# Batch 0's first loads on two queues: queries as fp32 by SP, keys as bf16 by POOL, and a new order of the first attention steps

## The chip, the cores and the metric

One Trainium2 chip, one core. The time is that of one execution on the device in microseconds; three runs are given by their median. Engines are called PE (TensorE), ACT (ScalarE), DVE (VectorE), POOL (GpSimd) and SP (SyncE); a load is issued by SP or by POOL and moved by the core's 16 DMA engines.

## The reference

Sliding-window attention over 8 batches of 8 heads, 576 positions of 64 elements, then two matrix products with a leaky ReLU between them:

```python
B, H, S, D = q.shape                      # 8, 8, 576, 64
scores = np.matmul(q, k.transpose(0, 1, 3, 2)) / np.sqrt(D)
mask = np.abs(pos[:, None] - pos[None, :]) <= 32
attn = softmax(np.where(mask, scores, -1e9))
x = np.matmul(attn, v).transpose(0, 2, 1, 3).reshape(B * S, H * D)   # 4608 x 512
h = x @ w_in                              # 512 x 2048
g = np.maximum(0.01 * h, h)
out = g @ w_out                           # 2048 x 512, float32
```

## The kernel before

Heads are worked in pairs, four pairs to a batch. For each pair, keys are laid out block-diagonally (`kbd`: head 0 in rows and columns 0 to 63, head 1 in 64 to 127, zeros elsewhere), so that one matmul serves both heads; values likewise in `vbd`. A step of attention is one pair and one half of the positions (288): five score matmuls into the PSUM tile `ps` (L296), an exponential on ACT (L301), the product with a 0/1 mask on POOL (L303, `prob`), row sums by a matmul with ones (L325, L328), their reciprocal on DVE (L333), five matmuls with the values (L347), and the scaling on DVE into `xT` (L361). Steps are numbered through: steps 0 to 3 are the four pairs of batch 0's first half, 4 to 7 its second half, and so on. After four steps 288 positions are ready for the first layer (`h_tile`, L375, and the activation at L382), and whole groups of 128 go through the second layer (`o_tile`, L417).

From batch 2 on, queries and keys are transposed by DMA, and a planner spreads the attention steps over the matmuls of the layers. Batches 0 and 1 are transposed on PE instead. The order of batch 0 is written out by hand (L481 to L532): each engine executes its instructions in the order of this text, so the place of a line decides what stands behind what in an engine's queue.

The queries and keys of batch 0 come by loads on POOL's queue that convert fp32 to bf16 on the way (`load_bf16`, L108): pairs 0 and 1 by themselves, pairs 2 and 3 in one load, queries and keys in turn. PE transposes them (L229), ACT evicts the queries into `qT` (L237). The keys of pairs 0 and 1 are evicted by ACT into `kT` (L250) and copied from there into `kbd` by DVE (`place_keys`, L279); those of pairs 2 and 3 go straight from PSUM into `kbd` by two ACT instructions (L245). The values come as fp32 by SP (L93, behind a small memset at L91) and are cast into `vbd` by POOL (L211) or ACT (L209). The parts of `kbd` and `vbd` that stay zero are cleared by DVE memsets (L143 to L147) and an ACT copy (L134).

`keep_busy` (L429) issues matmuls whose results nobody uses, so that PE doesn't stand still. The weights come by converting loads on POOL's queue (L475, L479). Batch 1's queries and keys are loaded by SP as fp32 (L79), behind a one-element memset on POOL (L75) that stands after the first two loads of w_out; they are cast to bf16 by DVE and POOL (L202) before PE transposes them (L232).

Of the kernel before, what the change touches and what calls it, by code (L numbers as in the profile page):

```python
# [9 lines left out]
FP32 = mybir.dt.float32  # L10
BF16 = mybir.dt.bfloat16
AF = mybir.ActivationFunctionType
# [4 lines left out]
def kernel(  # L17
# [14 lines left out]
    nc = tc.nc  # L32

    B, H, S, D = q.shape
# [52 lines left out]
    def load_v(b, p, behind=None):  # L87

        t = fload.tile([128, NB, D], FP32, name=f"vf{p}")
        if behind is not None:  # L90
            behind.memset(t[0:1, 0, 0:1], 0.0)  # L91
        for a in range(2):
            nc.sync.dma_start(  # L93
                out=t[64 * a:64 * a + 64],
                in_=v[b, 2 * p + a].rearrange("(c p) d -> p c d", p=64),
            )
        vf[b, p] = t
# [2 lines left out]
    kb = const.tile([96, NPAIR, RUN, 2, D], BF16)  # L100
    early = {}

    def load_bf16(p, n):

        for which, src in (("q", q), ("k", k)):
            t = (qb if which == "q" else kb)[:, p:p + n].rearrange("p n c a d -> p (n c a d)")
            t = t.rearrange("p (a c d) -> p a c d", c=RUN, d=D)
            nc.gpsimd.dma_start(  # L108
                out=t, in_=src[0, 2 * p:2 * (p + n)].rearrange("a (p c) d -> p a c d", c=RUN),
            )  # L110
            for i in range(n):
                early[which, p + i] = t[:, 2 * i:2 * i + 2]

    ident_f = const.tile([128, 128], FP32)
    make_identity(nc, ident_f)
    load_bf16(0, 1)
    load_bf16(1, 1)
    load_bf16(2, 2)
    ident = const.tile([128, 128], BF16)
    zero = const.tile([128, 1], BF16)  # L120
    nc.vector.memset(zero, 0.0)
# [10 lines left out]
    def clear(t, p):  # L132
        flat = t[:, p].rearrange("p n j -> p (n j)")
        nc.scalar.activation(  # L134
            out=flat, in_=zero.to_broadcast([128, NB * 128]), func=AF.Copy,
        )
# [5 lines left out]
    nc.vector.memset(win[0:64], 1.0)  # L142
    nc.vector.memset(kbd[0][:, 0:2], 0.0)  # L143
    nc.vector.tensor_copy(out=ident, in_=ident_f)
    nc.vector.memset(kbd[0][:, 2:4], 0.0)
    for p in range(1, NPAIR):
        nc.vector.memset(vbd[0][:, p], 0.0)  # L147

    WIN = [
        [((0, 0, 48), (2, 48, 64), (4, 112, 32)), ((1, 16, 64), (3, 80, 64))],  # L150
# [9 lines left out]
        out=w, in_=w, compare_op=ALU.is_ge, fill=0.0,  # L160
        base=2 * W, channel_multiplier=1, pattern=[[-1, 2], [0, 3], [-2, 64]],
    )
    win_f = win.rearrange("p c m i -> p c (m i)")

    def make_mask(hf):
# [12 lines left out]
        out=ps[:, 512:512 + HALF], in_=zero.to_broadcast([128, HALF]), func=AF.Copy,  # L178
    )
    clear(vbd[0], 0)  # L180


    RING = 4 * HALF
# [20 lines left out]
    def cast_v(b, p, eng=None, heads=range(2)):  # L204
        eng = eng or nc.gpsimd
        for a in heads:
            r = slice(64 * a, 64 * a + 64)
            if eng is nc.scalar:
                eng.activation(out=vbd[b % 2][r, p, :, r], in_=vf[b, p][r], func=AF.Copy)  # L209
            else:  # L210
                eng.tensor_copy(out=vbd[b % 2][r, p, :, r], in_=vf[b, p][r])  # L211
# [12 lines left out]
    def transpose(b, p, which):  # L224
        tp = mmps.tile([128, RUN, 96], BF16, name="tp", tag="mm")
        for c in range(RUN):
            if b == 0:
                for a in range(2):
                    nc.tensor.transpose(tp[64 * a:64 * a + 64, c], early[which, p][:, a, c], ident[0:96, 0:96])  # L229
            else:  # L230
                src = (qb if which == "q" else kb)[:, p, c].rearrange("p a d -> p (a d)")
                nc.tensor.transpose(tp[:, c], src, ident[0:96, 0:96])  # L232
        return tp

    def evict(b, p, which, tp, straight=False):
        if which == "q":
            nc.scalar.activation(  # L237
                out=qT[b][:, p].rearrange("p (c i e) -> p c i e", c=2, e=RUN // 2),
                in_=tp.rearrange("p (e c) i -> p c i e", c=2), func=AF.Copy,
            )  # L240
        elif straight:

            for a in range(2):
                r = slice(64 * a, 64 * a + 64)
                nc.scalar.activation(  # L245
                    out=kbd[b % 2][r, p, :, r], in_=tp[r].rearrange("p c i -> p i c"), func=AF.Copy,
                )
        else:
            kT = kt.tile([128, S], BF16, name="kT")
            nc.scalar.activation(  # L250
                out=kT.rearrange("p (i c) -> p i c", c=RUN),
                in_=tp.rearrange("p c i -> p i c"), func=AF.Copy,
            )
            unplaced.append((b, p, kT))

    def turn_over(b, p, which, straight=False):
        evict(b, p, which, transpose(b, p, which), straight)

    def transposes(b):

# [8 lines left out]
    def place_keys():  # L269

        while landing and landing[0][0] <= state["done"]:
            unplaced.append(landing.pop(0)[1:])
        while unplaced:
            b, p, kT = unplaced.pop(0)
            for a in range(2):
                r = slice(64 * a, 64 * a + 64)
                to = kbd[b % 2][r, p, :, r]
                if b < BY_DMA:
                    nc.vector.tensor_copy(out=to, in_=kT[r].rearrange("p (n j) -> p n j", j=64))  # L279
                else:  # L280
                    nc.vector.tensor_copy(  # L281
                        out=to.rearrange("p n (m c) -> p n c m", c=2),
                        in_=kT[r].rearrange("p (c n m) -> p n c m", c=2, n=NB),
                    )
# [6 lines left out]
    def score(i):  # L291
        b, hf, p = where(i)
        by_c = qT[b][:, p].rearrange("p (c i) -> p c i", c=2)
        for n_, blocks in enumerate(WIN[hf]):
            for blk, i0, n in blocks:
                nc.tensor.matmul(  # L296
                    ps_v[:, n_, :, i0:i0 + n], kbd[b % 2][:, p, blk],
                    by_c[:, :, hf * EVEN + i0:hf * EVEN + i0 + n], start=True, stop=True,
                )
        e = attn.tile([128, 2 * HALF], BF16, name="e")  # L300
        nc.scalar.activation(out=e, in_=ps[:, P0:P0 + 2 * HALF], func=AF.Exp, scale=scale)  # L301
        pr = prob[:, i % NPROB]
        nc.gpsimd.tensor_mul(  # L303
            pr.rearrange("p n c i -> p (n c i)"), e, mask[hf].rearrange("p n c i -> p (n c i)"),
        )
        probs[i] = [pr, None, None]
# [29 lines left out]
    def product(i, spare=False):  # L336

        b, hf, p = where(i)
        pr = probs[i][0]
        if spare:  # L340
            x = mmps.tile([128, 512], FP32, name="mm", tag="mm")[:, 0:HALF]
        else:
            x = xps.tile([128, HALF], FP32, name="x")
        x_v = x.rearrange("p (c i) -> p c i", c=2)
        parts = [(n_, *block) for n_ in range(2) for block in WIN[hf][n_]]
        for n_, blk, i0, n in parts:
            nc.tensor.matmul(  # L347
                x_v[:, :, i0:i0 + n], vbd[b % 2][:, p, blk, :], pr[:, n_, :, i0:i0 + n],
                start=(blk == parts[0][1]), stop=(blk == parts[-1][1]), skip_group_check=True,
            )  # L350
        probs[i][1] = x
# [7 lines left out]
    def scaled(i):  # L359
        _, x, r = probs.pop(i)  # L360
        nc.vector.tensor_mul(place(i), x, r)  # L361
# [63 lines left out]
    def keep_busy(t, lo, n):  # L425


        for _ in range(n):
            nc.tensor.matmul(  # L429
                t[:, lo:lo + 224], ones_bd, mask[0].rearrange("p n c i -> p (n c i)")[:, 0:224], start=False, stop=False,  # L430
                skip_group_check=True,
            )
# [41 lines left out]
    def load_w_in(f0, f1):  # L474
        nc.gpsimd.dma_start(out=w_in_bf[:, :, f0:f1], in_=w_in_r[:, :, f0:f1])  # L475
# [3 lines left out]
        nc.gpsimd.dma_start(out=w_out_bf[:, c, :], in_=w_out_r[:, c, :])  # L479

    qT[0] = attn.tile([128, NPAIR, S], BF16, name="qT")  # L481
    turn_over(0, 0, "q")
    turn_over(0, 0, "k")
    place_keys()
    for p in range(NPAIR):
        load_v(0, p, nc.vector if p == 0 else None)
    nc.vector.tensor_copy(out=win[64:128], in_=win[0:64])
    make_mask(0)
    turn_over(0, 1, "q")
    turn_over(0, 1, "k")  # L490
    score(0)
    place_keys()
    make_mask(1)
    turn_over(0, 2, "q")
    score(1)
    tq3 = transpose(0, 3, "q")
    turn_over(0, 2, "k", True)
    sums(0)
    evict(0, 3, "q", tq3)
    tk3 = transpose(0, 3, "k")  # L500
    keep_busy(ps, 0, 6)
    sums(1, True)
    load_w_in(0, 512)
    load_w_in(512, 1024)
    score(2)
    evict(0, 3, "k", tk3, True)
    keep_busy(ps, 0, 6)
    cast_v(0, 0, None, (0,))
    cast_v(0, 0, nc.scalar, (1,))
    cast_v(0, 1, None, (0,))  # L510
    cast_v(0, 1, nc.scalar, (1,))
    cast_v(0, 2, None, (0,))
    sums(2)
    score(3)
    product(0)
    product(1, True)
    scaled(0)
    scaled(1)
    cast_v(0, 2, nc.scalar, (1,))
    load_w_in(1024, 1536)  # L520
    keep_busy(ps, 0, 6)
    score(4)
    product(2)
    scaled(2)
# [149 lines left out]
```

## Time and profile before

| | |
|---|---|
| median of 3 runs | 321.42 us (321.33 to 322.27) |
| the profiled execution | 321.34 us, span of the instructions 319.6 us |
| batch 0's first query pair landed | 4.93 us |
| first score matmul | 9.46 us |
| first matmul of the first layer | 22.83 us |
| first issue of batch 1's loads | 26.51 us |

Times inside the run are microseconds from the start of the span. In a timeline a row is: start, duration, engine, line, operation, output <- input, and the number of instructions merged into it; in brackets the idle time of the engine ahead of it and what ended that. In a list of waits the three numbers are the total, how often, and the longest. PEld is PE's loading of weights, which runs beside its matmuls.

### The profile page before, as it was taken

Reading aid. Unit: us, or ns where it says so; the run is one execution under the profiler, and the core shown is the slowest. Engines: PE = TensorE matmul, PEld = TensorE weight load, DVE = VectorE, ACT = ScalarE, POOL = GpSimd, SP = SyncE. Lnnn points to the kernel's source line nnn. Section 1 sums busy time; section 2 is a strip of 40 time slices with the busy share of each in tenths; the row PEclk is TensorE's granted clock in tenths of the full one; section 3 lists DMA queues with packets and bytes.
Section 4 is the critical chain, followed back from the end, with each engine's and each line's share of the span. In section 5 each row is a group of like instructions: output and inputs, shape, how many; then the busy total and the mean of one; then the engine's idle time right before and its main releaser. Section 6 shows DMA issues by size and latency. Waiting matters only on the chain.

```text
span 319.6 us, 6565 instructions
## 1 busy us (share of the span) xinstructions
PE 305.3 (96%) x2498; PEld 205.7 (64%) x2498; DVE 216.2 (68%) x263; ACT 180.6 (56%) x391; POOL 187.5 (59%) x246
## 2 busy tenths in 40 slices
PE   1889988999999999999999999999999999999995
PEld 1677764576765858576765858576765858576753
DVE  6678645869755997688755997688755987565100
ACT  5677688574652828374552828365552828463631
POOL 7579845974646866586646866586646866330000
PEclk9999999999999999999999999999999999999999
DMA  6999999996999999399834998399733520000101
GB/s 86 191 154 175 267 254 210 242 218 144 214 246 182 226 245 180 77 206 231 177 74 95 262 191 177 77 243 207 162 76 106 113 63 35 35 35 7 61 33 67
DMA packets 108368, 48.28 MB, mean 151 GB/s; under 512 B 68784, under 2 KB 103856, under 8 KB 108336
## 3 DMA queue, kind: packets, MB, share of 16 engines
q1 hardware_dynamic: 102480, 42.48, 64.3%
q0 software_dynamic: 5856, 5.37, 11.1%
q8 instruction: 19, 0.31, 0.4%
q14 instruction: 13, 0.11, 0.1%
HBM read 36.70 MB, written 9.44 MB: 144 GB/s over the span
## 4 chain that ended last, share of the span: by engine, by line
PE 84%; DMA 8%; POOL 3%; SPq 1%; ACT 1%; issue 1%; DVE 1%; POOLq 0%; ACTq 0%; DVEq 0%
PE mm L417 37%; PE mm L375 34%; DMA kf<-in_k_dram 6%; PE x L347 4%; PE ps L296 4%; DMA qb<-in_q_dram 2%; PE s L325 2%; SPq L79 1%; POOL prob L303 1%; PE tp L229 1%; DVE r L333 1%; POOL w_in_bf L475 0%; POOL w_out_bf L479 0%; POOL qb L108 0%; ACT vbd L209 0%
## 5 line engine op out<-in xcount | busy, mean ns | idle before, releaser
L333 DVE RECIPROCAL r<-s 128x288 f32<-128x288 f32 x63 | 123.3, 1956 | 58.8 <-PE s L325 53.4
L303 POOL TENSOR_TENSOR prob<-e,mask 128x576 bf16<-128x576 bf16 x64 | 81.5, 1273 | 92.0 <-ACT e L301 45.4
L375 PE MATMUL mm<-xT,w_in_bf 128*128 128x288 bf16 x1024 | 134.0, 286 | 0.3
L417 PE MATMUL mm<-w_out_bf,gT 128*128 128x512 bf16 (+2 forms) x592 | 130.4, 373 | 0.2 <-DMA w_out_bf<-in_moe_w_out_dram 0.2
L382 ACT ACTIVATE gT<-mm 128x288 bf16<-128x288 f32 x256 | 101.2, 411 | 24.9 <-PE mm L375 8.4
L375 PEld LDWEIGHTS <-w_in_bf 128*128 128x128 bf16 x1024 | 98.4, 98 | 24.8 <-issue 0.6
L417 PEld LDWEIGHTS <-gT 128*128 128x128 bf16 x592 | 56.4, 98 | 59.6 <-issue 0.3
L422 ACT ACTIVATE o_sb<-mm 128x512 f32<-128x512 f32 (+2 forms) x37 | 21.7, 585 | 92.0 <-PE mm L417 92.0
L301 ACT ACTIVATE e<-ps 128x576 bf16<-128x576 f32 x64 | 41.5, 648 | 10.5 <-PE ps L296 10.3
L211 POOL CAST vbd<-vf 64x576 bf16<-64x576 f32 x51 | 35.1, 689 | 1.4
L202 POOL CAST kb<-kf 96x384 bf16<-96x384 f32 (+1 forms) x52 | 30.5, 608 | 5.7 <-DMA kf<-in_k_dram 5.7
L361 DVE TENSOR_TENSOR xT<-x,r 128x288 bf16<-128x288 f32 x63 | 28.8, 457 | 7.1 <-PE x L347 0.8
L281 DVE COPY kbd<-kT 64x576 bf16<-64x576 bf16 x48 | 32.3, 673 | 0.7 <-DMA kT<-kb 0.3
L296 PEld LDWEIGHTS <-kbd 128*128 128x128 bf16 x320 | 21.2, 100 | 8.9
L296 PE MATMUL ps<-qT,kbd 128*128 128x128 bf16 (+2 forms) x320 | 26.7, 216 | 0.0
L347 PE MATMUL x<-prob,vbd 128*128 128x64 bf16 (+1 forms) x315 | 25.6, 213 | 0.6 <-ACT vbd L209 0.4
L202 POOL CAST qb<-qf 96x384 bf16<-96x384 f32 x48 | 24.4, 536 | 0.0
L347 PEld LDWEIGHTS <-vbd 128*128 128x128 bf16 x320 | 20.8, 99 | 3.1 <-ACT vbd L209 0.7
L313 DVE TENSOR_TENSOR both<-prob 128x288 bf16<-128x288 bf16 x52 | 19.8, 382 | 0.9
L325 PE MATMUL s<-both,ones_bd 128*128 128x288 bf16 x52 | 14.9, 286 | 0.0
L229 PE MATMUL tp<-ident,qb 96*64 96x96 bf16 x48 | 2.8, 282 | 7.5 <-DMA qb<-in_q_dram 7.5
L209 ACT ACTIVATE vbd<-vf 64x576 bf16<-64x576 f32 x13 | 8.8, 680 | 0.3
(56 smaller groups left out, 86.3 us busy)
## 6 DMA issues: line engine op xcount, KB each, us to landing
vf<-in_v_dram SPq DMA_DIRECT2D x64, 144.0 KB, 4.5
out_dram<-o_sb SPq DMA_DIRECT2D x35, 256.0 KB, 4.0
qf<-in_q_dram SPq DMA_DIRECT2D x28, 288.0 KB, 4.7
kf<-in_k_dram SPq DMA_DIRECT2D x28, 288.0 KB, 5.1
w_in_bf<-in_moe_w_in_dram POOLq DMA_DIRECT2D x4, 512.0 KB, 6.7
w_out_bf<-in_moe_w_out_dram POOLq DMA_DIRECT2D x4, 512.0 KB, 16.3
qT<-qb SPq DMA_TRANSPOSE x24, 4.1
kT<-kb SPq DMA_TRANSPOSE x24, 3.2
```

What stands on the lines that cost most here:

```text
L202: eng.tensor_copy(out=to, in_=tok)
L211: eng.tensor_copy(out=vbd[b % 2][r, p, :, r], in_=vf[b, p][r])
L281: nc.vector.tensor_copy(out=to.rearrange("p n (m c) -> p n c m", c=2), in_=kT[r].rearrange("p (c n m) -> p n c m", c=2, n=NB),)
L296: nc.tensor.matmul(ps_v[:, n_, :, i0:i0 + n], kbd[b % 2][:, p, blk], by_c[:, :, hf * EVEN + i0:hf * EVEN + i0 + n], start=True, stop=True,)
L301: nc.scalar.activation(out=e, in_=ps[:, P0:P0 + 2 * HALF], func=AF.Exp, scale=scale)
L303: nc.gpsimd.tensor_mul(pr.rearrange("p n c i -> p (n c i)"), e, mask[hf].rearrange("p n c i -> p (n c i)"),)
L333: nc.vector.reciprocal(r, s)
L347: nc.tensor.matmul(x_v[:, :, i0:i0 + n], vbd[b % 2][:, p, blk, :], pr[:, n_, :, i0:i0 + n], start=(blk == parts[0][1]), stop=(blk == parts ...
L361: nc.vector.tensor_mul(place(i), x, r)
L375: nc.tensor.matmul(h[:, 0:HALF], w_in_bf[:, c, ts(f, 128)], xT[:, c, ds(g * HALF % RING, HALF)], start=(c == 0), stop=(c == DMC - 1),)
L382: nc.scalar.activation(out=gT[:, f, ds(g * HALF % RING, HALF)].rearrange("p (i c) -> p i c", c=2), in_=h[:, 0:HALF].rearrange("p (c i) -> ...
L417: nc.tensor.matmul(o[:, lo:hi], gT[:, f, ds(128 * j % RING, 128)], w_out_bf[:, f, lo:hi], start=(f == 0), stop=(f == FFC - 1),)
```

## The change

Batch 0's queries are no longer converted by the load. Four loads on SP's queue, one for each pair, bring them as fp32 into `qf`, and a new function `cast_q` casts them into `qb`: pairs 0 to 2 on DVE, pair 3 on POOL. The keys stay converting loads on POOL's queue, now one for each pair. Queries are therefore transposed with both heads in one instruction, keys as before one head at a time.

All keys of batch 0 go straight from PSUM into `kbd` (`straight`), pairs 0 and 1 by ACT and DVE with one head each, pairs 2 and 3 by ACT alone. Clearing moves: DVE clears `kbd`'s pairs 2 and 3 after the first query cast; `vbd`'s pair 1 goes to ACT, its pairs 2 and 3 to POOL.

The order of the first steps changes: the sums of step 0 stand ahead of the last transposes, the casts of values move to other engines and places, w_in's first load is issued after step 0 and its second after step 2, and three of the calls of `keep_busy` issue four matmuls instead of six.

```diff
-    def load_bf16(p, n):
-        for which, src in (("q", q), ("k", k)):
-            t = (qb if which == "q" else kb)[:, p:p + n].rearrange("p n c a d -> p (n c a d)")
-            t = t.rearrange("p (a c d) -> p a c d", c=RUN, d=D)
-            nc.gpsimd.dma_start(
-                out=t, in_=src[0, 2 * p:2 * (p + n)].rearrange("a (p c) d -> p a c d", c=RUN),
-            )
-            for i in range(n):
-                early[which, p + i] = t[:, 2 * i:2 * i + 2]
+    def load_early(p):
+        t = fload.tile([96, 2, RUN * D], FP32, name=f"qf{p}")
+        nc.sync.dma_start(out=t, in_=q[0, 2 * p:2 * p + 2].rearrange("a (p c) d -> p a (c d)", c=RUN))
+        qf[0, p] = t
+        t = kb[:, p].rearrange("p c a d -> p (c a d)").rearrange("p (a c d) -> p a c d", c=RUN, d=D)
+        nc.gpsimd.dma_start(out=t, in_=k[0, 2 * p:2 * p + 2].rearrange("a (p c) d -> p a c d", c=RUN))
+        early[p] = t
...
-    load_bf16(0, 1)
-    load_bf16(1, 1)
-    load_bf16(2, 2)
+    for p in range(NPAIR):
+        load_early(p)
...
-    nc.vector.memset(kbd[0][:, 2:4], 0.0)
-    for p in range(1, NPAIR):
-        nc.vector.memset(vbd[0][:, p], 0.0)
...
+    nc.gpsimd.memset(vbd[0][:, 2], 0.0)
+    nc.gpsimd.memset(vbd[0][:, 3], 0.0)
...
     clear(vbd[0], 0)
+    clear(vbd[0], 1)
...
+    def copy(eng, out, in_):
+        if eng is nc.scalar:
+            eng.activation(out=out, in_=in_, func=AF.Copy)
+        else:
+            eng.tensor_copy(out=out, in_=in_)
+
+    def straight(p, tp, *engs):
+        for a, eng in enumerate(engs):
+            r = slice(64 * a, 64 * a + 64)
+            copy(eng, kbd[0][r, p, :, r], tp[r].rearrange("p c i -> p i c"))
+
+    def cast_q(p, eng):
+        copy(eng, qb[:, p], qf[0, p].rearrange("p a (c d) -> p c a d", d=D))
...
+    ACT, DVE, POOL = nc.scalar, nc.vector, nc.gpsimd
+    cast_q(0, DVE)
     turn_over(0, 0, "q")
-    turn_over(0, 0, "k")
-    place_keys()
+    tk0 = transpose(0, 0, "k")
+    DVE.memset(kbd[0][:, 2:4], 0.0)
+    cast_q(1, DVE)
+    straight(0, tk0, ACT, DVE)
+    turn_over(0, 1, "q")
     for p in range(NPAIR):
-        load_v(0, p, nc.vector if p == 0 else None)
-    nc.vector.tensor_copy(out=win[64:128], in_=win[0:64])
+        load_v(0, p, DVE if p == 0 else None)
+    cast_q(2, DVE)
+    cast_q(3, POOL)
+    DVE.tensor_copy(out=win[64:128], in_=win[0:64])
     make_mask(0)
-    turn_over(0, 1, "q")
-    turn_over(0, 1, "k")
     score(0)
-    place_keys()
+    straight(1, transpose(0, 1, "k"), ACT, DVE)
+    turn_over(0, 2, "q")
     make_mask(1)
-    turn_over(0, 2, "q")
+    load_w_in(0, 512)
     score(1)
-    tq3 = transpose(0, 3, "q")
-    turn_over(0, 2, "k", True)
     sums(0)
-    evict(0, 3, "q", tq3)
+    straight(2, transpose(0, 2, "k"), ACT, ACT)
+    turn_over(0, 3, "q")
     tk3 = transpose(0, 3, "k")
-    keep_busy(ps, 0, 6)
+    keep_busy(ps, 0, 4)
     sums(1, True)
-    load_w_in(0, 512)
+    cast_v(0, 0, POOL, (0,))
+    score(2)
+    keep_busy(ps, 0, 4)
+    straight(3, tk3, ACT, ACT)
+    cast_v(0, 0, POOL, (1,))
     load_w_in(512, 1024)
-    score(2)
-    evict(0, 3, "k", tk3, True)
-    keep_busy(ps, 0, 6)
-    cast_v(0, 0, None, (0,))
-    cast_v(0, 0, nc.scalar, (1,))
-    cast_v(0, 1, None, (0,))
-    cast_v(0, 1, nc.scalar, (1,))
-    cast_v(0, 2, None, (0,))
     sums(2)
     score(3)
     product(0)
+    scaled(0)
+    cast_v(0, 1, ACT)
+    cast_v(0, 2, ACT, (0,))
+    cast_v(0, 2, POOL, (1,))
     product(1, True)
-    scaled(0)
     scaled(1)
-    cast_v(0, 2, nc.scalar, (1,))
     load_w_in(1024, 1536)
-    keep_busy(ps, 0, 6)
+    keep_busy(ps, 0, 4)
     score(4)
     product(2)
     scaled(2)
```

More of the change, by code (lines that the diff above doesn't have):

```diff
@@ L226, in transpose @@
         for c in range(RUN):
-            if b == 0:
+            if b == 0 and which == "k":
                 for a in range(2):
-                    nc.tensor.transpose(tp[64 * a:64 * a + 64, c], early[which, p][:, a, c], ident[0:96, 0:96])
+                    nc.tensor.transpose(tp[64 * a:64 * a + 64, c], early[p][:, a, c], ident[0:96, 0:96])
             else:
@@ L233, in transpose, with evict @@
         return tp
-    def evict(b, p, which, tp, straight=False):
+    def copy(eng, out, in_):
[9 more added lines that the diff above has]
+        copy(eng, qb[:, p], qf[0, p].rearrange("p a (c d) -> p c a d", d=D))
+    def evict(b, p, which, tp):
         if which == "q":
@@ L240, in evict @@
             )
[L241 to L247, printed above, removed]
         else:
@@ L254, in evict, with turn_over @@
             unplaced.append((b, p, kT))
-    def turn_over(b, p, which, straight=False):
-        evict(b, p, which, transpose(b, p, which), straight)
+    def turn_over(b, p, which):
+        evict(b, p, which, transpose(b, p, which))
     def transposes(b):
```

## The prediction

> **What bounds the kernel now.** The page's first part says which engine carries the run: PE is busy for 305.3 of 319.6 us, so a gain or loss must be PE time that is empty or slow now.
>
> ```profile
> PE 305.3 (96%) x2498; PEld 205.7 (64%) x2498; DVE 216.2 (68%) x263; ACT 180.6 (56%) x391; POOL 187.5 (59%) x246
> ```
>
> The list of PE's waits says where it is empty:
>
> ```profile
> PE tp L229 <- DMA qb<-in_q_dram: 7.5, 3, 5.0
> PE tp L232 <- POOL kb L202: 1.1, 2, 0.9
> PE ps L429 <- ACT e L301: 0.8, 1, 0.8
> PE x L347 <- ACT vbd L209: 0.4, 1, 0.4
> PE mm L417 <- DMA w_out_bf<-in_moe_w_out_dram: 0.2, 1, 0.2
> ```
>
> The first row is the 7.5 us that the change is about: batch 0's transposes waiting for queries. The second, fourth and fifth rows lie between 44 and 52 us: 0.89 + 0.20 + 0.44 + 0.21 = 1.74 us in which PE waits for batch 1's keys and values and the last of w_out. After that it waits no more, and every microsecond of shift reaches the end. So the prologue's end counts only as far as those transfers come earlier too. The chain that ended last shows what releases them: POOL's weight loads, POOL's small memset at L75, SP's issues at L79, and the last key load.
>
> ```profile
> 24.93 1.49 POOL w_out_bf L479 x2
> 26.42 0.07 POOL qf L75
> ...
> 30.45 17.78 DMA kf<-in_k_dram
> ```
>
> The engines' timelines, 16 to 27 us, give the steps from the third score on:
>
> ```profile
> 16.16 0.66 PE L296 MATMUL ps<-qT,kbd 128*128 128x96 bf16 x5
> 17.62 1.28 PE L429 MATMUL ps<-mask,ones_bd 128*128 128x224 bf16 x6 [0.80 <-ACT e L301]
> 20.31 0.66 PE L347 MATMUL mm<-prob,vbd 128*128 128x96 bf16 x5
> 21.55 0.40 PE L296 MATMUL ps<-qT,kbd 128*128 128x64 bf16 x5
> ```
>
> ```profile
> 18.78 1.25 ACT L209 ACTIVATE vbd<-vf 64x576 bf16<-64x576 f32 x2
> 20.16 0.65 ACT L301 ACTIVATE e<-ps 128x576 bf16<-128x576 f32 x1
> ```
>
> ```profile
> 17.65 1.27 POOL L303 TENSOR_TENSOR prob<-e,mask 128x576 bf16<-128x576 bf16 x1 [1.83 <-ACT e L301]
> 18.87 1.87 POOL L211 CAST vbd<-vf 64x576 bf16<-64x576 f32 x3
> 20.89 1.27 POOL L303 TENSOR_TENSOR prob<-e,mask 128x576 bf16<-128x576 bf16 x1
> 22.11 0.80 POOL L475 DMA_DIRECT2D w_in_bf<-in_moe_w_in_dram  x1
> ```
>
> To be seen here: ACT's and POOL's casts of the values fill the hole between one exponential and the next; five score matmuls take 0.66 us at first and 0.40 from 21.55 on, so PE runs at about half speed until some 21.15; and from 20.89 to SP's first issue at 26.51 POOL hardly pauses.
>
> **Part by part: the loads.** Six issues on POOL (0.63 to 0.82 each) become four, ended by 4.3 instead of 5.6. SP issues four fp32 query loads, 0.4 to 0.5 each (as L79), from about 0.8, when the other engines start. The eight pair loads of before moved packets from 3.3 (POOL's first issue at 1.58 plus 1.7) to the landing at 12.70: 9.4 us. From SP the stream can start at about 2.4.
> Does a second queue add speed? The windows by time show the engines already full: DMA share 1.12 at 6 to 8 us with POOL's queue alone, 1.15 at 38 to 40 us with both. So 9.4 us of work from 2.4 ends at 11.8: 0.9 us won, not half the time.
> How the two queues share isn't shown for this pair. If SP's stream goes first, the last query lands at 2.4 + 9.4/2 = 7.1; if last, at 11.8. In the packet records of 34 to 44 us the two queues advance packet for packet (about 110 each per us). With 1.2 us alone at the start, that puts the last query at some 9.6, the first keys at 5.6 (5.73 now). I take this.
>
> **Casts, evictions, memsets.** New are four casts of queries: three on DVE (0.56 alone, 1.24 beside a POOL memset, by L202) and one on POOL (0.82). The first keys go from PSUM to kbd by ACT's half (0.65, as L245) beside DVE's half. No row has that DVE copy: 0.46 is half of L279's pair out of SBUF, 0.92 twice L361's 288 columns out of PSUM; PSUM being the source, I take 0.75. ACT's eviction and DVE's two copies go (0.65 + 0.91 and two handovers), so the first score moves from 9.46 to about 8.1. DVE's moved memsets lie in its waits for data; two vbd memsets of 1.0 to 1.2 each go to POOL, whose queue ends them at about 7.7, before the last query lands. Should that landing be 7.1, they cost up to 0.6.
>
> **The new wait.** cast_q(3) stands on POOL ahead of the first probability product, and everything queued behind that: w_in's first issue, the second product, the casts of values. The sum, with the last query at 9.6: cast to 10.45, first product to 11.72 (10.93 to 12.20 now). sums(0) now stands ahead of the last three groups of transposes, so PE waits for that product with all of them behind it: sums(0) at 11.8, 0.5; three groups at 0.6, to 14.1; four keep_busy at 0.18 (1.09 for six now), to 14.8; sums(1) 0.48; score(2) at **15.3** instead of 16.16, a gain of 0.9. With the last query at 7.1, masks and score(1) bound instead: 14.2 or a little less. With 11.8: 17.5.
>
> **What follows score(2).** It sets the exponential of score(3) to end 4.65 us later, as now (20.81 − 16.16). But the casts of pair 1's values, done by 20.1 now, stand behind that exponential on ACT: two at 0.68, so product(1) runs 6.05 after score(2), not 4.15. PE queues keep_busy, score(4), product(2) and the first h matmul behind it. On POOL, one more cast (0.66) stands behind the fourth product, and the fifth waits for score(4): product 1.27 from 4.73, cast to 6.64, w_in's issue to 7.44; score(4) at 7.23 with PE slow, its exponential to 8.63, product to 10.0, w_in to 10.8, two w_out issues to 12.3, memset, SP's issue at 12.4 (11.6 with PE fast), against 10.35 now. Batch 1's first load is thus issued at 15.3 + 12.4 = 27.7 instead of 26.51: **1.2 us late**; with PE fast, 0.4. The idle DMA engines of now (share 0.44 at 22 to 24 us) get a second hole, since w_in's last quarter is issued at 25.3, not 24.14.
>
> **PE's speed.** PE is unbroken from 17.62 and speeds up 3.5 us later. After the change it stops for 1.9 us ahead of product(1) (21.35), so I count those 3.5 us from there, to 24.85: 3.5 us at half speed instead of 0.84, a loss of 1.3 us. Bounds: 0 if the stop doesn't count, 3.0 if another such stretch is needed.
> The Trainium skill (TensorE: Matmul & The Clock Gate, section "Part 1: The HAM clock gate (the "warmup" mystery)") has full speed come after a sustained busy window of about 3.4 us. The trace's 17.62 to 21.15 agrees, but 11.04 to 16.83 was as unbroken and released nothing; by the rule alone the sums after 11.8 could release it before the stop, and PE's sum below would be 0.9 instead of 2.2; the forecast would stay, since the transfers are later than either.
>
> **The sum on PE:** product(1) later by 21.35 − 20.31 = 1.04, two keep_busy fewer −0.19, half speed +1.33: first layer 2.2 later. The waits of 1.74 absorb that down to 0.4, but only if the transfers are no later; they are late by up to 1.2, and the chain of waits has them last. I take 1.2. On the profiled execution's 321.34 (span 319.6 and 1.74 around it) this is 322.54; the median of the runs is 0.08 higher: **322.6**.
>
> **The rivals.**
> *Queries first, faster:* SP's stream is served ahead of the keys, so POOL's cast leaves early, and sums(0) ahead of the transposes starts the chain early. It decides from score(2) before 14.3 on with PE fast by product(2): at 13.5 the load issue is at 13.5 + 11.6 = 25.1, 1.4 early, and PE's own sum is under the waits: 320.0. For it: SP starts 0.8 us ahead of POOL. Against: the packet-for-packet sharing, and score(1) behind mask and cast on DVE.
> *Hidden both ways, no change:* batch 1's first packet comes 4.4 us after its issue now, behind w_in's last quarter; a later issue may just wait less, and PE's loss goes into the 1.74: 321.5.
> *Late queries:* the last query at 11.8, or a second slow stretch of PE (2.2 + 1.7 − 1.74): 323.4 to 324.8; say 324.
>
> **How the numbers follow.** My forecast 0.38, late queries 0.12, no change 0.27, queries first 0.23. A measurement of this kernel can tell about 0.3%, 1 us. The forecast lies near that edge, so 0.03 of it goes to "same": slower 0.47, same 0.30, faster 0.23. The range reaches from near the fast rival to near the late one: 320.1 to 324.0; the forecast's own is 322.0 to 323.4.
>
> **What would show it.** Right: cast_q(3) waiting on POOL for a load until 9 to 10.5; score(2) near 15.3; PE idle nearly 2 us ahead of product(1), ended by ACT's cast; five-matmul groups still at 0.66 there; SP's batch-1 issue after 27; waits between 44 and 52 us shrunk. Wrong: cast_q(3) before 8.5, score(2) before 14.3, or SP's issue before 26.5.

## The result, and the profile after

The changed kernel takes **324.51 us** (median of 5 executions, 323.54 to 325.16) against 321.53 for the kernel before beside it: ratio 1.0087, 95% interval 1.0062 to 1.0112. It is slower by 3 us. The profiled execution took 323.54 (span 321.8), the shortest of the five, so the trace explains 2.2 of the 3 us; the rest lies in executions without a trace.

PE is busy for about as long as before (304.6 us for 305.3), so the loss is again empty or slow PE time.

```profile
PE 304.6 (95%) x2448; PEld 206.2 (64%) x2468; DVE 218.2 (68%) x261; ACT 181.4 (56%) x392; POOL 190.7 (59%) x247
```

The list of PE's waits (in total, times, longest):

```profile
PE tp L229 <- DVE qb L236: 4.4, 1, 4.4
PE tp L226 <- DMA kb<-in_k_dram: 2.0, 1, 2.0
PE ps L301 <- DVE kbd L236: 1.9, 2, 0.9
PE mm L352 <- ACT vbd L206: 1.6, 1, 1.6
PE x L352 <- ACT vbd L206: 0.9, 1, 0.9
```

The wait for queries is shorter, but three new ones stand below it: for keys, for DVE's half of their copy into `kbd`, and for ACT's cast of the values. After 44 us PE waits once, 0.94 us (the last line), where it waited 1.74 before. PE's timeline (start, length, work, and in brackets the idle time ahead of it):

```profile
7.04 0.69 PE L226 MATMUL tp<-ident,kb 96*64 96x96 bf16 x12 [1.98 <-DMA kb<-in_k_dram]
...
9.27 0.64 PE L301 MATMUL ps<-qT,kbd 128*128 128x96 bf16 x5 [0.94 <-DVE kbd L236]
...
16.14 0.66 PE L301 MATMUL ps<-qT,kbd 128*128 128x96 bf16 x5
...
22.11 0.63 PE L352 MATMUL mm<-prob,vbd 128*128 128x96 bf16 x5 [1.62 <-ACT vbd L206]
...
27.34 0.66 PE L301 MATMUL ps<-qT,kbd 128*128 128x64 bf16 x5
...
29.35 0.40 PE L301 MATMUL ps<-qT,kbd 128*128 128x64 bf16 x5
```

The first keys are turned at 7.04, not 5.78; the third score is where it was (16.16); product(1) comes 1.8 us later than before, behind a stop of 1.62; five score matmuls still take 0.66 us at 27.34, so PE is slow some 7 us longer. The other engines:

```profile
7.77 0.64 ACT L234 ACTIVATE kbd<-tp 64x576 bf16<-64x576 bf16 x1 [2.02 <-PE tp L226]
...
20.14 0.65 ACT L306 ACTIVATE e<-ps 128x576 bf16<-128x576 f32 x1 [1.41 <-PE ps L301]
20.69 2.08 ACT L206 ACTIVATE vbd<-vf 64x576 bf16<-64x576 f32 x3
```

```profile
8.45 0.76 DVE L236 COPY kbd<-tp 64x576 bf16<-64x576 bf16 x1 [1.85 <-ACT kbd L234]
9.25 1.09 DVE L236 CAST qb<-qf 96x768 bf16<-96x768 f32 x1
...
10.81 0.22 DVE L165 COPY mask<-win 128x256 bf16<-128x256 bf16 x1
```

```profile
9.11 0.82 POOL L236 CAST qb<-qf 96x768 bf16<-96x768 f32 x1
11.19 1.27 POOL L308 TENSOR_TENSOR prob<-e,mask 128x576 bf16<-128x576 bf16 x1 [1.26 <-DVE mask L165]
```

```profile
0.81 1.88 SPq L106 DMA_DIRECT2D qf<-in_q_dram  x4
...
28.44 0.32 SPq L79 DMA_DIRECT2D qf<-in_q_dram  x1
```

POOL's cast of the last queries hardly waited for their load: the load was there at 9.05, and POOL's memsets had ended at 9.00. The first product waited for DVE's mask, which stood behind the copy of the late keys and the cast of the third queries. DVE's half of that copy started only when ACT's half had ended (8.45, behind 7.77 + 0.64). SP issues batch 1's first load at 28.44 instead of 26.51. The steps side by side, each from the two profiled executions:

| start of, us | before | after | later by |
|---|---|---|---|
| first keys' transposes | 5.78 | 7.04 | 1.26 |
| score(2) | 16.16 | 16.14 | −0.02 |
| product(1) | 20.31 | 22.11 | 1.80 |
| first layer's first matmul | 22.83 | 25.42 | 2.59 |
| first layer's 25th matmul (PE fast in both by then) | 28.29 | 31.57 | 3.28 |
| first matmul with w_out | 45.70 | 47.81 | 2.11 |
| end of the span | 319.6 | 321.8 | 2.2 |

From the first matmul with w_out to the end it is 273.9 us in one and 274.0 in the other: what separates these two executions is decided before 48 us.

### The profile page after: what moved, and what is told of

Its sections match the earlier page's. It is cut to its first block, busy times and chain, and to the rows that moved or that the text cites. A ratio compares the mean times of both kernels' runs of the same rounds, so it can differ in the third digit from the quotient of the medians.

```text
span 321.8 us, 6484 instructions
## 1 busy us (share of the span) xinstructions
PE 304.6 (95%) x2448; PEld 206.2 (64%) x2468; DVE 218.2 (68%) x261; ACT 181.4 (56%) x392; POOL 190.7 (59%) x247
## 4 chain that ended last, share of the span: by engine, by line
PE 90%; ACT 2%; DVE 2%; DMA 2%; issue 2%; POOL 1%; POOLq 0%; ACTq 0%; DVEq 0%
PE mm L380 39%; PE mm L422 38%; PE ps L301 5%; PE x L352 5%; PE s L330 2%; DMA kb<-in_k_dram 2%; DVE r L338 1%; PE s L333 1%; ACT vbd L206 1%; POOL prob L308 1%; ACT e L306 1%; PE tp L229 1%; DVE kbd L236 0%; ACT kbd L234 0%; PE ps L434 0%
## 5 line engine op out<-in xcount | busy, mean ns | idle before, releaser
L422 PE MATMUL mm<-w_out_bf,gT 128*128 128x512 bf16 (+2 forms) x572 | 128.7, 373 | 1.1
L229 PE MATMUL tp<-ident,qb 96*128 96x96 bf16 x48 | 4.3, 241 | 4.4 <-DVE qb L236 4.4
```

The lines of the kernel that those rows point to most:

```text
L422: nc.tensor.matmul(o[:, lo:hi], gT[:, f, ds(128 * j % RING, 128)], w_out_bf[:, f, lo:hi], start=(f == 0), stop=(f == FFC - 1),)
```

## The experiments

Theory at the start: the casts of pairs 1 and 2 ahead of product(1) make the stop, the slow PE and the late issues (**casts**). Rival: the two load streams share the DMA engines otherwise than forecast, and the late keys cost the time (**loads**). The table gives the profiled execution of each kernel (start of the first keys' transposes, score(2), product(1), SP's first load of batch 1, first matmul with w_out, PE's waits after 40 us) and then the medians of all executions.

| kernel | keys | score(2) | product(1) | SP | w_out | waits | profiled us | median us | ratio, 95% |
|---|---|---|---|---|---|---|---|---|---|
| before | 5.78 | 16.16 | 20.31 | 26.51 | 45.70 | 1.74 | 321.34 | 321.45 to 321.77 | 1 |
| after | 7.04 | 16.14 | 22.11 | 28.44 | 47.81 | 0.94 | 323.54 | 324.51 | 1.0062 to 1.0112 |
| e1 casts ahead | 8.13 | 17.23 | 21.38 | 27.88 | 46.86 | 1.87 | 323.27 | 324.44 | 1.0074 to 1.0132 |
| e2 before, casts late | 5.68 | 16.43 | 22.09 | 28.77 | 47.78 | 1.11 | 323.52 | 323.50 | 1.0035 to 1.0083 |
| e3 stop filled | 8.56 | 17.66 | 23.64 | 29.54 | 48.31 | 1.31 | 324.09 | 324.19 | 1.0076 to 1.0118 |
| e4 old loads | 5.65 | 15.70 | 21.01 | 27.33 | 46.30 | 1.74 | 322.68 | 322.54 | 1.0011 to 1.0044 |
| e6 keys first | 6.93 | 16.10 | 22.07 | 28.40 | 46.94 | 0.91 | 322.95 | 322.98 | 1.0035 to 1.0080 |
| e7 old loads, casts ahead | 5.89 | 15.29 | 19.45 | 26.26 | 44.66 | 1.46 | 320.93 | 321.56 | 0.9987 to 1.0017 |
| e8 keys first, casts ahead | 6.94 | 16.04 | 20.19 | 26.97 | 45.29 | 1.46 | 325.97 | 323.44 | 1.0039 to 1.0096 |
| e9 e7, w_in earlier | 5.73 | 15.56 | 19.36 | 26.77 | 45.67 | 1.38 | 321.30 | 321.07 | 0.9967 to 0.9998 |
| e11 one queue | 6.63 | 18.16 | 24.14 | 30.46 | 49.35 | 1.37 | 325.00 | 324.97 | 1.0077 to 1.0134 |
| e12 e9, more w_in earlier | 5.83 | 16.19 | 20.25 | 26.71 | 45.52 | 2.07 | 322.02 | 320.88 | 0.9962 to 0.9996 |
| e13 before, split loads | 8.19 | 18.31 | 22.09 | 28.32 | 47.32 | 1.45 | 323.75 | 324.47 | 1.0068 to 1.0117 |
| e14 first query alone | 5.16 | 14.54 | 18.34 | 25.06 | 43.59 | 2.47 | 320.38 | 320.39 | 0.9938 to 0.9972 |

**Casts or loads.** e1 is the changed kernel with ACT's casts of pair 1 and POOL's of pair 2 moved ahead of sums(2):

```diff
+    cast_v(0, 1, ACT)
     load_w_in(512, 1024)
+    cast_v(0, 2, POOL, (1,))
     sums(2)
     score(3)
     product(0)
     scaled(0)
-    cast_v(0, 1, ACT)
     cast_v(0, 2, ACT, (0,))
-    cast_v(0, 2, POOL, (1,))
```

> The changed kernel with the casts of pair 1's values ahead of step 3's exponential on ACT, and POOL's cast of pair 2 ahead of step 3's product; all else stays. Theory 'casts': the changed kernel loses because product(1) waits 1.6 us behind ACT's casts and PE stays at half speed until 28 us after that stop. Then product(1) comes 4.2 us after score(2), at about 20.4 instead of 22.11, PE is fast by 22 to 25, the first layer starts near 23, and the time falls by 2 to 3 us, to 321.5 to 322.5. Theory 'loads': the late first keys and the later loads of weights and of batch 1 set the end; the time stays within 0.7 us of the changed kernel's 324.5. Theory 'fewer keep_busy': PE stays slow because of the holes behind the four keep_busy; product(1) moves but PE is slow until 25 or later, and less than half comes back, 323.2 or more.

e2 is the kernel before with nothing but the place and the engines of those casts taken from the change:

```diff
-    cast_v(0, 1, None, (0,))
-    cast_v(0, 1, nc.scalar, (1,))
-    cast_v(0, 2, None, (0,))
     sums(2)
     score(3)
     product(0)
-    product(1, True)
     scaled(0)
+    cast_v(0, 1, nc.scalar)
+    cast_v(0, 2, nc.scalar, (0,))
+    cast_v(0, 2, None, (1,))
+    product(1, True)
     scaled(1)
-    cast_v(0, 2, nc.scalar, (1,))
```

> The kernel before, with nothing of the change but the place of the casts of pairs 1 and 2's values: behind product(0), pair 1 by ACT alone, as in the changed kernel. Theory 'casts': product(1) moves from 20.3 to about 22.1, PE stops nearly 2 us, stays slow to about 28, and the time is 2 to 3 us above before: 323.5 to 324.5. Theories 'loads' and 'fewer keep_busy': less than 0.8 us above before, under 322.3, since the waits of 1.74 us between 44 and 52 us absorb it.

In the old kernel the casts cost 2.05 us (323.50 against 321.45), with a stop of 1.83 us, as forecast. In the changed kernel undoing them gains nothing that can be measured: 324.44. The stop is gone in e1's PE timeline, yet its keys landed later still, and a wait for w_out takes the place of the stop:

```profile
8.13 0.69 PE L226 MATMUL tp<-ident,kb 96*64 96x96 bf16 x12 [2.74 <-DMA kb<-in_k_dram]
...
21.38 0.66 PE L352 MATMUL mm<-prob,vbd 128*128 128x96 bf16 x5
...
51.55 1.02 PE L422 MATMUL mm<-w_out_bf,gT 128*128 128x512 bf16 x4 [0.81 <-DMA w_out_bf<-in_moe_w_out_dram]
```

So the casts alone do not explain the change. e3 leaves the casts where the change has them and fills the stop, nine `keep_busy` matmuls into unused columns of product(1)'s tile:

```diff
     product(0)
+    x1 = mmps.tile([128, 512], FP32, name="mm", tag="mm")
+    keep_busy(x1, HALF, 9)
...
-    product(1, True)
+    product(1, x=x1)
```

> The changed kernel with nine more keep_busy matmuls between product(0) and product(1), into unused columns of product(1)'s PSUM tile: the stop stays, but PE works through it (9 x 0.19 = 1.7 us). It prices PE's speed apart from the wait. Theory 'casts' with the speed as its larger part: product(1) stays at 22.1, PE is fast from 22 to 25 instead of 28, and 1 to 2 us of the 3.0 come back: 322.5 to 323.5. If the wait alone counted, the time stays at 324.5 within 0.5 us. Theory 'loads': also unchanged.

PE is fast earlier, as meant: from product(1) to the first layer's 25th matmul it takes 7.68 us, against 9.46 in the changed kernel and 7.98 before. The time barely moves (324.19); in the profiled execution the keys came 1.5 us later again. e4 takes the other side, the old bf16 loads of the queries on POOL's queue in turn with the keys, without the casts of queries, all else as changed:

```diff
-        nc.sync.dma_start(out=t, in_=q[0, 2 * p:2 * p + 2]...)      # fp32, by SP
-        nc.gpsimd.dma_start(out=t, in_=k[0, 2 * p:2 * p + 2]...)
+        for which, src, dst in (("q", q, qb), ("k", k, kb)):
+            nc.gpsimd.dma_start(out=t, in_=src[0, 2 * p:2 * p + 2]...)
```

> The changed kernel with batch 0's queries loaded again as bf16 on POOL's queue, one load for each pair, in turn with the keys, and no casts of queries; order, evictions, casts of values and keep_busy stay as changed. Theory 'casts': score(2) moves by less than 0.7 us, the stop ahead of product(1) stays, the time is within 0.8 us of 324.5. Theory 'loads': the first keys land at 5.7 again instead of 7.0, and 1.5 us or more come back, to 323 or less.

That gives back 2.0 us. e7 is e4 with e1's edit:

> The changed kernel with batch 0's queries loaded as bf16 on POOL's queue and no casts of queries, and besides with the casts of pairs 1 and 2's values ahead of step 3 (the edits of two earlier runs together). Theory 'two losses': with the keys early and the stop gone, the place of the casts is worth what it costs in the kernel before, 1 to 2 us: 320.8 to 321.6, product(1) at about 20.0. Theory 'transfers set the end': without the stop PE waits again between 44 and 52 us, and less than 0.5 us comes back of 322.5.

With both undone, 321.56: as before. So the new order of evictions, sums and transposes costs nothing in the sum, and the loss is that of the two parts, which do not add: with the casts ahead the loads cost 2.9 us (e1 less e7), with the casts late 2.0; the casts cost 1.0 beside the old loads (e4 less e7) and nothing measurable beside the new ones.

**What it is about the loads.** e13 is the kernel before with the loads alone changed:

```diff
-    load_bf16(0, 1)
-    load_bf16(1, 1)
-    load_bf16(2, 2)
+    for p in range(NPAIR):
+        load_early(p)          # fp32 query by SP, bf16 key by POOL
...
+    cast_q(0, nc.vector)
     turn_over(0, 0, "q")
     turn_over(0, 0, "k")
     place_keys()
+    cast_q(1, nc.vector)
     (load_v)
+    cast_q(2, nc.vector)
+    cast_q(3, nc.gpsimd)
```

> The kernel before with one part of the change alone: batch 0's queries as four fp32 loads on SP's queue beside the keys as bf16 on POOL's, with the casts of queries 0 to 2 on DVE and 3 on POOL; evictions, order of sums and casts of values stay as before. If SP's stream is served ahead of the keys and this is what the loads cost, the first keys land at 7.0 to 8.5 (5.8 before), score(2) comes at 17 to 18 (16.16), SP's first load of batch 1 is issued at 27.3 to 28.4 (26.51), and the time is 322.3 to 323.4. If the two queues share one to one, as forecast, or the loss is in the order of the steps, the keys land by 6.2 and the time is 321.0 to 321.8.

The loads, with the casts that they need, cost all that the change does: 1.0093. Keys and SP's issue lie where the loads theory had them; score(2) and the time are later than it said. In the trace the second cast stands behind the keys' copies on DVE, and PE waits for it (the releaser named is the one-element memset that runs into that cast):

```profile
8.19 0.69 PE L226 MATMUL tp<-ident,kb 96*64 96x96 bf16 x12 [0.81 <-DMA kb<-in_k_dram]
11.15 0.66 PE L229 MATMUL tp<-ident,qb 96*128 96x96 bf16 x6 [2.28 <-DVE vf L91]
```

e6 holds SP's stream back: the changed kernel with the queries of pairs 1 to 3 issued at about 2.0 us instead of 1.2.

```diff
     nc.vector.memset(win[0:64], 1.0)
+    for p in range(1, NPAIR):
+        load_early_q(p, nc.vector if p == 1 else None)   # behind a memset of one element
```

> The changed kernel, but the query loads of pairs 1 to 3 wait on SP behind a one-element DVE memset, so that they are issued from 2.0 us on instead of 1.2, and the first keys, issued by POOL from 1.58, find fewer queries ahead of them. Bytes, casts, queues and all other orders stay. Theory 'queue order': the loss against the version with old loads (2.0 us) is the first keys' landing, 7.0 to 8.5 us behind queries that nobody needs yet; then they land by 6.2, the first score starts by 8.8, score(2) by 15.8, and about 2 us come back: 322 to 323. Theory 'fp32 queries': the casts on DVE and POOL and the larger writes are the cost; then the time stays above 323.7.

The time, 322.98, is in the expected range, 1.5 us better than the change; the landing is not (6.93 where 6.2 was expected), and score(2) is no earlier. The queries' share did change: 50 and 88 of SP's packets per us at 3 to 5 us, 172 and 151 in the changed kernel. But between the two profiled executions, 0.6 us apart, it is the clock that differs for PE: product(1) starts at 22.07 and 22.11, while full speed is granted at 25.15 instead of 27.97, and the first layer's 25th matmul runs at 30.53 instead of 31.57. So this trace doesn't show that the order of the loads gave the time back; the medians say that holding the queries back pays 1.5 us, and how it does so is open. e8 adds e1's edit to it:

> The changed kernel with the query loads of pairs 1 to 3 held back to 2.0 us and the casts of pairs 1 and 2's values ahead of step 3: both suspected losses taken away, all else as changed. Theory 'two losses': 320.8 to 321.8, no slower than the kernel before. Theory 'transfers set the end': the loads of weights are issued later than before, so the waits between 44 and 52 us return and the time stays at 322 or more.

It missed: 323.44. Its profiled execution lost some 5 us far behind the prologue: DVE waited 2.95 us, until 117.44, for a later batch's keys from their DMA transpose, PE then stood 2.03 us for DVE, and its granted clock was at half for 3.4 us from 123 us on. Its prologue is early enough (w_out at 45.29). The other executions spread from 321.4 to 326.4, and what spoils those is open.

e11 puts the same fp32 loads on POOL's queue, in turn with the keys:

```diff
-        nc.sync.dma_start(out=t, in_=q[0, 2 * p:2 * p + 2]...)
+        nc.gpsimd.dma_start(out=t, in_=q[0, 2 * p:2 * p + 2]...)
```

> The changed kernel with its four fp32 query loads issued on POOL's queue, in turn with the key loads (q0, k0, q1, k1, ...), instead of on SP's; bytes, tiles and the four casts of queries stay. If the loss of the loads comes from SP's stream being served ahead of POOL's, the first keys land by 6.2 (7.0 to 8.5 with the two queues), the first score is at 9.2 or before, score(2) within 16.1, and the time is 322.3 to 323.2, near that of the bf16 loads (322.5). If it comes from the fp32 bytes in SBUF and the casts of queries on DVE and POOL, the keys' landing alone does not help: 323.7 to 324.8, as the changed kernel (324.4 to 324.5).

Neither theory had this right. The keys came in time (turned at 6.63, behind the queries, with no wait), but now the queries were late, and their casts stand in the way of other work. DVE's and POOL's timelines:

```profile
8.85 1.59 DVE L236 CAST qb<-qf 96x768 bf16<-96x768 f32 x1 [1.67 <-DMA qf<-in_q_dram]
10.47 0.76 DVE L236 COPY kbd<-tp 64x576 bf16<-64x576 bf16 x1
```

```profile
11.94 0.85 POOL L236 CAST qb<-qf 96x768 bf16<-96x768 f32 x1 [1.91 <-DMA qf<-in_q_dram]
13.17 1.27 POOL L308 TENSOR_TENSOR prob<-e,mask 128x576 bf16<-128x576 bf16 x1 [0.38 <-DVE mask L165]
```

DVE's half of the first keys' copy stands behind the cast of the second queries; the first product stands behind the cast of the last. The time, 324.97, lies just above what the fp32 theory had (323.7 to 324.8); e6, with the same bytes and casts at 322.98, speaks against these as the whole cost. A cast puts the landing into an engine's order, where a converting load holds up PE alone.

**Better versions.** e14 keeps the part of the idea that pays: e7 with the first pair of queries alone as fp32 by SP.

```diff
+        if p == 0:
+            t = fload.tile([96, 2, RUN * D], FP32, name="qf0")
+            nc.sync.dma_start(out=t, in_=q[0, 0:2]...)
...
+    cast_q(0, DVE)
     turn_over(0, 0, "q")
```

> The kernel with bf16 loads and the casts of values ahead of sums(2) (321.56), but with the first pair of queries alone as fp32 on SP's queue and cast on DVE; the other seven pair loads stay bf16 on POOL's queue in turn. If it is the length of SP's stream (four loads) that holds the keys back, one load of 288 KB takes some 1.1 us of the engines at 253 GB/s and is over by 4.0, the first keys land at 5.2 to 5.8, the first score is at 8.0 to 8.6 (8.61), SP's first load of batch 1 is issued at 25.6 to 26.3 (26.26) and the time is 320.3 to 321.3. If any fp32 query on SP's queue costs what the four do (first keys after 6.5, more work on DVE), it is 322 or more.

320.39, ratio 0.9955: faster than both kernels. One load is all but over (its last packet ends at 3.25 us) when POOL's stream begins (3.12), the first keys are earlier than in any other kernel here, and SP's issue comes 1.45 us before that of the kernel before. PE's timeline shows what is late next, the end of w_out:

```profile
5.16 0.69 PE L230 MATMUL tp<-ident,kb 96*64 96x96 bf16 x12 [0.25 <-DMA kb<-in_k_dram]
...
7.39 0.63 PE L305 MATMUL ps<-qT,kbd 128*128 128x96 bf16 x5 [0.76 <-DVE kbd L240]
...
49.12 1.02 PE L426 MATMUL mm<-w_out_bf,gT 128*128 128x512 bf16 x4 [1.16 <-DMA w_out_bf<-in_moe_w_out_dram]
```

e9 and e12 tried the weights' transfers on top of e7. e9 issues w_in's second quarter before score(2), e12 also the third ahead of POOL's half cast of pair 2's values:

```diff
     cast_v(0, 0, POOL, (0,))
+    load_w_in(512, 1024)                 # e9
     score(2)
...
     cast_v(0, 1, ACT)
-    load_w_in(512, 1024)
+    load_w_in(1024, 1536)                # e12
     cast_v(0, 2, POOL, (1,))
```

> As the version with old loads and casts ahead, and besides w_in's second quarter is issued on POOL ahead of step 2's product, where POOL idles about 2 us, instead of behind it (about 15.5 instead of 19). Theory 'transfers set the end': the DMA engines' idle stretch around 20 us is filled, the last weights and batch 1's values come about 1 us earlier, and the time falls by 0.5 to 1 us against the version without it, below 321. Otherwise no change within 0.3 us.

> The kernel with bf16 loads, casts of values ahead of sums(2) and w_in's second quarter issued before score(2), with the third quarter of w_in moved ahead of POOL's half cast of pair 2's values, where POOL waited 1.57 us for the values' load, so that the DMA engines' idle stretch from 22 to 25 us is filled. If the transfers of the weights and of batch 1's loads set the end (waits of PE between 44 and 55 us: 1.4 us in the kernel without this move), their shift by 1 to 2 us brings the waits below 0.8 and the time to 320.2 to 320.8, under the kernel before (321.45). If the end is set by PE alone, or if the weight transfer only delays the values' load and with it product(2), it stays at 321.0 to 321.6.

Both are slightly under the kernel before (0.9982 and 0.9979, each interval just below 1). e9 is 0.5 us under e7, at the low end of what was expected, but not below 321, and its interval overlaps e7's. e12 missed its range by a little, 320.88 for 320.2 to 320.8, and its waits did not shrink: its profiled execution, the slowest of its runs, has 2.07 us of them. SP's issue stayed at 26.71 (26.77 in e9), and the idle stretch of the DMA engines (share 0.30 at 22 to 24 us in e9) became a shallower one later on (0.78 and 0.82 at 24 to 28).

## Why the prediction was wrong

It said slower, which it is; but 322.6 was 1.9 us too low, and 324.5 lies half a microsecond outside the range. About 1.0 us of the 1.9 is in the profiled execution (2.2 over that of before, where 1.2 was forecast); the rest is that the other executions ran longer than the profiled one, and they have no trace. By its steps:

**The sharing of the queues failed, and most else follows from it.** "The two queues advance packet for packet ... the last query at some 9.6, the first keys at 5.6. I take this." The row was from 34 to 44 us and does not hold at the start. In the changed kernel's packet records SP's queue begins at 1.84 us (2.4 in the forecast) and starts 190, 172 and 151 packets at 2 to 5 us; POOL's 0, 3 and 50, where POOL's queue alone, in the kernel before, started 100 and 256 at 3 to 5. The last query was there at 9.05, near the 9.6 forecast, but the first keys only at 7.0, and at 8.1 to 8.6 in the profiles of e1, e3 and e13, which load alike. That the other executions of the changed kernel, 0.7 to 1.6 us longer than the profiled one, had such later keys fits this, but they have no trace.

**The wait on POOL was named at the wrong place.** The cast of the last queries ran at 9.11, right behind POOL's memsets (to 9.00, forecast 7.7), and the product followed at 11.19, not for the cast but for a mask behind DVE's copy of the late keys. That copy was forecast as two halves beside each other; DVE's half ran behind ACT's, 0.68 us later than beside it, and so it did in all the kernels here that split a copy in this way, starting 0.03 us or so after ACT's end (7.30 behind 6.63 + 0.65 in e7) unless a cast held it longer, as once in e11. What makes it wait the traces don't show beyond naming ACT's copy. e11 shows the mechanism as forecast, at the forecast's late bound: cast at 11.94 for 11.8, score(2) at 18.16 for 17.5. But there it is POOL's own queue that is late.

**score(2)** was put at 15.3, by the last query, and came at 16.14, by the first keys: in the changed order with all four queries on SP it starts 9.10 us after their transposes whether these start at 7.04, 8.13 or 8.56 (after, e1, e3; 9.17 in e6, 9.10 in e8). So the 0.9 us to be won was lost to the keys. With old loads it came at 15.29 to 16.19 (e7, e4, e9, e12).

**What follows score(2)** was right. product(1) is 5.97 behind it (6.05 forecast), ended by ACT's cast after a stop of 1.62 (nearly 2). SP's issue is 12.30 behind it (12.4), but from the later score: 28.44 for 27.7.

**PE's speed** was mis-sized, inside its bounds of 0 and 3.0. The 3.5 us were counted from the end of the stop, to 24.85, a loss of 1.33. The clock goes by fixed stretches of 3.41 us instead (last section): the one from 21.14 to 24.55 still holds 0.97 us of the stop and released nothing; the next, busy throughout, did.

```profile
21.14:24.55 3.41, 2.44 (x21) 2.25 (x22) 1.32 (x4) 2.08 (x4) 2.48 (x3) 1.00 1.05 155
24.55:27.97 3.42, 3.42 (x21) 2.44 (x19) 2.31 (x2) 1.39 (x3) 3.13 (x4) 1.00 1.06 156
```

(The windows of the changed kernel: length, then busy time of PE, PEld, DVE, ACT and POOL with their instructions, granted clock, DMA share, GB/s. The clock's column knows nothing ahead of the first record, here at 27.97, and shows 1.00; the matmuls' durations tell.) From product(1) to the first layer's 25th matmul PE needs 9.46 us for 7.98, with two `keep_busy` fewer that hide 0.19: a loss of 1.67. The sum on PE, forecast as 1.04 − 0.19 + 1.33 = 2.2, is 1.80 − 0.19 + 1.67 = 3.28.

**The transfers last** was wrong for the profiled execution. Of the 3.28, 1.17 were absorbed up to the first matmul with w_out (0.89 of it the wait for batch 1's keys, which is gone); the later waits stayed (0.85 before, 0.94 now), ended by ACT's cast of values and not by a transfer, and the chain of waits runs through PE there. That is 2.2 us where 1.2 was taken. So the direction is in part luck: it was to come from late transfers, with PE's own sum absorbed down to 0.4, and in the trace it came from PE's sum. In e1 and e14, where PE is earlier, the wait for w_out is there (0.81 and 1.16 us): both limits lie close to each other, which may be why the parts do not add.

**The rivals.** "Queries first, faster" had the event right and its sign wrong: SP's stream was served ahead, but a score needs the keys as well, and the two orders only choose which of them is late. "Late queries" came nearest with its 324, by luck: the last query landed at 9.05 and not at 11.8, and the second slow stretch of PE did come (24.55 to 27.97) but made the loss 1.67 instead of 1.33 us, not 1.7 more.

## What to carry to other kernels

Here a row of two queues in steady state said nothing on who is served first while both start: where the first work needs one tile from each stream, bound the other tile's landing by the whole of the first stream. Give the second queue the one load that is needed first, and no more: here it gained 1.2 us by the medians (e14 to e7), while four such loads lost 2 to 3. A cast in place of a converting load makes the casting engine wait for the landing in its own order, so list what stands behind each.

## What the runs showed of the hardware

**SP's queue, once started, held back POOL's, which starts later.** POOL's converting loads moved their first packet at 3.1 us where SP issued nothing or a single load before them (before, e2, e4, e7, e9, e11, e12, e14), but at 3.4 to 5.1 beside SP's four (3.39 in e6 and 3.58 in e8, which hold three of them back; 3.78 after, 4.33 in e13, 4.95 in e3, 5.06 in e1), with POOL's first issue at 1.6 in all of them. The Trainium skill (DMA: Bandwidth & Descriptors, section "Queues, rings and completion order") has each DMA engine take turns between its queues by the packet, typically 9 to 17 descriptors. From 5 us on the two queues advance about one to one in the trace's packets (94 to 118, then 121 to 109, per us in the changed kernel); before that they don't, and why is not settled here.

**PE's clock is judged by fixed windows.** The records of granted clock change only in steps of 3.41 us. In e4 (columns as above):

```profile
12.35:15.76 3.41, 3.41 (x47) 2.51 (x45) 1.96 (x1) 2.59 (x4) 2.15 (x3) 1.00 1.21 181
15.76:19.17 3.41, 1.72 (x21) 1.21 (x20) 2.40 (x2) 1.96 (x4) 2.14 (x3) 1.00 1.15 209
19.17:22.58 3.41, 1.95 (x19) 1.55 (x18) 2.29 (x3) 2.44 (x4) 3.22 (x4) 0.50 0.73 89
22.58:26.00 3.42, 3.42 (x22) 2.49 (x20) 1.90 (x2) 1.90 (x3) 2.27 (x3) 0.50 1.19 184
```

The window in which PE is busy throughout (12.35 to 15.76) is followed by full speed; the one with PE busy for 1.72 us by half speed, before the stop ahead of product(1) has even begun; 1.95 while slow doesn't release it, the next full window does, at 26.00. e2, e12 and e14 show the same (full speed after 3.41, taken back after 1.81, 1.72 and 1.76). Speed that is won early can so be lost again, for 3.4 us in e12 and e14 and for 6.8 in e2 and e4. The Trainium skill (TensorE: Matmul & The Clock Gate, section "Part 1: The HAM clock gate (the "warmup" mystery)") says that the window is free-running and doesn't start with the work; the steps agree. So the place of a stop between the windows counts: 0.97 us of the changed kernel's stop lies in the window that ends at 24.55, which released nothing, but only 0.33 us of e6's in the one that ends at 25.15, which did. PE's busy time is not the whole measure, though. Among windows at half speed without transposes, those with 2.96 us (e7) or more released full speed and those with 2.67 (e8) or less did not. With transposes in them it doesn't sort: 3.22 released it in e9 (11.83 to 15.24), but 3.27 did not (10.90 to 14.31 in the kernel before, mostly transposes), nor even 3.41 in e1 (14.11 to 17.53) and e3 (14.22 to 17.63), whose next score, at 20.47 and 20.90, still takes 0.66 us. And 1.81 in e9 (15.24 to 18.66) didn't take it back, as 1.81 in e2 did. What is counted stays open.

**DVE's casts stretch beside POOL.** The same fp32 cast of 96x768 took 0.56 us alone, 1.13 beside POOL's select for `win`, 1.09 beside POOL's own cast, and 1.59 in e11 beside POOL's memset. The select stretched too: 1.90 us there, 0.54 in the kernel before.
